# ScalarE's order in a step of an attention kernel: the postmix weights ahead of the copy of the postmix

## The chip, the cores and the metric

One core of one Trainium2 chip. The metric is the time of one execution on the device in microseconds (us); of several executions the median counts.

## What is computed

An attention with two mixes over the heads (2 batches, 12 heads, 448 tokens, 64 channels), then two dense blocks (768 to 2048 to 768) over its 896 rows. The attention is the part that matters here:

```python
scores = scale * np.matmul(q, k.transpose(0, 1, 3, 2))
scores = np.einsum('bhij,hg->bgij', scores, w_pre)
scores = scores - np.max(scores, axis=-1, keepdims=True)
attn = np.exp(scores)
attn = attn / (np.sum(attn, axis=-1, keepdims=True) + 1e-09)
attn = np.einsum('bhij,hg->bgij', attn, w_post)
return np.matmul(attn, v).astype(np.float32)
```

All of it is in float32; products that need it are made of three matmuls over a high and a low part of each operand.

## The kernel before

The attention runs over 8 chunks, four in each batch, three of 120 query rows and one of 88. A chunk is cut into groups of 10 rows x 12 heads = 120 partitions: 12 groups in a long chunk, 9 in a short one, 90 in all. One turn of the loop over groups is a **step**; there are 90, counted by `m`. The order of the work inside a step is written out by hand (a manual schedule), and every engine takes its instructions in that order. In step m stand:

- GpSimd (POOL): `gsplit(m + 2)` (L273 and L275) splits the scores of group m+2 into `sh` and `sl`. Two buffers each, so `sh` of group m+2 follows the matmuls of group m.
- TensorE (PE): `premix(m)` (L285 to L287), three matmuls into the bank `M`; then `postmix(m - 2)` (L320), eight records of matmuls into the bank `A`, whose stationary operand is `e` of group m-2 and whose moving operand is `wr` of group m-2; then, by tables over the steps of a chunk, two heads' scores of the next chunk (L254, bank `sc`), or two heads' product with v of the chunk before (L340, bank `X`), or both, or neither.
- VectorE (DVE): the row maximum of `M` (L289), and for group m-1 the sum's reciprocal (`norm`, L299 and L300), which lands in `st`.
- ScalarE (ACT): `e` = exp of `M` with the maximum as its bias, and the row sums (L291, two records); the copy `at` of the postmix of group m-3 out of its bank (L324; `aposts` holds it from the step before); and `weigh(m - 2)` (L304), the postmix weights divided by the row sum: `wr` = `wq` times the reciprocal of group m-2.

ScalarE has besides these a copy of one `sc` bank (L257), the copies of `X` (L356), and in some steps preparations of q and k (L229, L221), moves of x (L477) and the first piece of a dense block's weights (L408). DVE takes the other half of each (L257, L357, L230, L222, L410 to L416). In the step's text the copy `at` comes first, then `wr`, then the rest; exp stands at the end of what a step hands to ScalarE, apart from the preparations behind it.

The scores of the next chunk go through a staging tile and a DMA on SP's queue (`spread`, L239) into `full`, from which `gsplit` reads; the first `gsplit` of a chunk, two steps ahead of the chunk's first step, needs the DMAs of all heads.

`A` and `M` have two banks each, `wr` two buffers, `e` four. After the loop, the last two groups are finished in a tail written out by hand, with copy and weights in an order of its own.

Of the kernel before, what the change touches and what calls it, by code (L numbers as in the profile page):

```python
# [49 lines left out]
def fused_kernel(  # L50
# [63 lines left out]
    def load_q(C):  # L114
        ns = chunks[C][3] * GR
        t = front.tile([128, NP, CH], F32, tag="qraw", bufs=2, name=f"qraw{C}")
        nc.sync.dma_start(out=t[:, :, :ns], in_=q[C, :, :, :ns])
        qraw[C] = t

    def load_k(b, m):  # L120
        t = front.tile([128, 2, S], F32, tag="raw", bufs=5, name=f"kraw{b}_{m}")
        nc.sync.dma_start(out=t, in_=k[b, :, 2 * m : 2 * m + 2])
        kraw[(b, m)] = t

    def load_v(C, hp):
        if C < len(chunks) - 1:
            t = att.tile([JP, 2, JC * D], F32, tag="vraw", bufs=3, name=f"vraw{C}_{hp}")
            nc.sync.dma_start(out=t, in_=v[chunks[C][0], hp])
            vraw[(C, hp)] = t
# [87 lines left out]
    def k_prep(b, hp):  # L217
        src = kraw[(b, hp // 2)][:, hp % 2, :]
        hi, lo = kst[:, 0, hp, :], kst[:, 1, hp, :]
        preps.append([  # L220
            lambda: nc.scalar.activation(out=hi, in_=src, func=AF.Copy),  # L221
            lambda: nc.vector.tensor_tensor(out=lo, in0=src, in1=hi.bitcast(F32), op=ALU.subtract),  # L222
        ])

    def q_prep(C, p0=0, p1=NP):
        ns = chunks[C][3] * GR
        hi, lo, src = (x[:, p0:p1, :ns] for x in (qr, ql, qraw[C]))
        preps.append([
            lambda: nc.scalar.activation(out=hi, in_=src, func=AF.Copy),  # L229
            lambda: nc.vector.tensor_tensor(out=lo, in0=src, in1=hi.bitcast(F32), op=ALU.subtract),  # L230
        ])
# [9 lines left out]
    def scores(C, hp, tags=("sc", "sc"), st=None):  # L241
        n = chunks[C][3] * GR
        kh, kl = kst[:, 0, hp, :], kst[:, 1, hp, :]
        if hp == 0:
            full[C] = att.tile([GP, MG, S], F32, tag="full", bufs=2, name=f"full{C}")
        room(2)
        sc = [ps.tile([128, 512], F32, tag=t, bufs=BUFS[t], name=f"sc{C}_{2 * hp + i}") for i, t in enumerate(tags)]
        far = st is None
        if far:
            st = front.tile([CH, 2, S], F32, tag="raw", bufs=5, name=f"stg{C}_{hp}")  # L250
        for j, (w, x) in enumerate(((qr, kh), (ql, kh), (qr, kl))):
            for i in range(2):
                o = slice(i * D, i * D + D)
                nc.tensor.matmul(sc[i][:n, :S], lhsT=w[o, hp, :n], rhs=x[o], start=(j == 0), stop=(j == 2))  # L254

        def take(i, copy):
            copy(out=st[:n, i], in_=sc[i][:n, :S])  # L257
            if far:
                spread(C, 2 * hp + i, st[:, i])

        post(2, lambda: take(0, nc.scalar.copy), lambda: take(1, nc.vector.tensor_copy))
# [3 lines left out]
    def gsplit(m, eng=nc.gpsimd):  # L265
        if m >= len(groups):
            return
        C, g = groups[m]
        r = GP
        sh = att.tile([GP, S], F32R, tag="sh", bufs=2, name=f"sh{m}")  # L270
        sl = att.tile([GP, S], F32R, tag="sl", bufs=2, name=f"sl{m}")
        s = full[C][:, g, :]
        eng.tensor_scalar(out=sh[:r], in0=s[:r], scalar1=1.0, scalar2=0.0, op0=ALU.mult, op1=ALU.add)  # L273
        ssp[m] = (sh, sl)
        return eng.tensor_tensor(out=sl[:r], in0=s[:r], in1=sh[:r].bitcast(F32), op=ALU.subtract)  # L275
# [20 lines left out]
    def norm(m):  # L296
        r = GP
        e, st = epx[m]
        nc.vector.tensor_scalar(out=st[:r, 2:3], in0=st[:r, 1:2], scalar1=1e-9, scalar2=None, op0=ALU.add)  # L299
        nc.vector.reciprocal(out=st[:r, 3:4], in_=st[:r, 2:3])  # L300

    def weigh(m):
        wr = att.tile([GP, H, GR], F32, tag="wr", bufs=2, name=f"wr{m}")
        nc.scalar.activation(out=wr, in_=wq, func=AF.Copy, scale=epx[m][1][:, 3:4])  # L304
        wrs[m] = wr
# [23 lines left out]
    def av_unit(C, h):  # L329
        b, r0, n, G = chunks[C]  # L330
        if h % 2 == 0:
            return
        if h % 4 == 1:
            tag = "X" if C + 1 < len(chunks) or h == 1 else "A"
            xps[C] = ps.tile([128, 512], F32, tag=tag, bufs=BUFS[tag], name=f"X{C}_{h}")
        X = xps[C][:, : 2 * CH].rearrange("p (h n) -> p h n", n=CH)
        for jc in range(JC):
            for hh in (h - 1, h):
                vs = vraw[(C, hh // 2)][:, hh % 2, :].rearrange("p (c d) -> p c d", d=D)
                nc.tensor.matmul(  # L340
                    X[hh % 2 * D : hh % 2 * D + D, hh % 4 // 2, :n], lhsT=vs[:, jc, :], rhs=at[C][:, jc, hh, :n],
                    start=(jc == 0), stop=(jc == JC - 1),
                )
        load_v(*((C, h // 2 + 3) if h // 2 + 3 < NP else (C + 1, h // 2 + 3 - NP)))
        if h % 4 == 3:
            av_evac(C, h, X)
# [178 lines left out]
    LAG = 2  # L525
# [8 lines left out]
    m = 0  # L534
    for C, (b, r0, n, G) in enumerate(chunks):
        nxt = C + 1 if C + 1 < len(chunks) else None
        sched = {}

        def add(units, steps):
            for i, u in enumerate(units):  # L540
                sched.setdefault(steps[i * len(steps) // len(units)], []).append(u)

        if nxt is not None:
            add([lambda h=h: scores(nxt, h) for h in range(NP)], SST[G])
        if C + 2 < len(chunks):
            add([lambda: q_prep(C + 2, 0, NP // 2), lambda: q_prep(C + 2, NP // 2, NP)], QST[G])
        if C == NCH - 2:
            add([lambda m=m: load_k(1, m) for m in range(3)], [4, 5, 6])
            add([lambda h=h: k_prep(1, h) for h in range(NP - 1)], [8, 8, 9, 10, 11])
        if C == NCH - 1:  # L550
            add([lambda: k_prep(1, NP - 1)], [0])
        if C > 0:
            add([lambda h=h: av_unit(C - 1, h) for h in range(1, H, 2)], [("av", a) for a in AVST[G]])

        for s in range(G):
            if s == 0 and C + 2 < len(chunks):
                load_q(C + 2)
            if C == 0 and s == 1:
                for i in range(3):
                    load_v(0, i)  # L560
            while aposts:
                aposts.pop(0)()
            if m >= LAG:
                weigh(m - LAG)
            for p in posts + xposts:
                p[0]()
            gsplit(m + 2)
            for p in posts:
                p[1]()
            premix(m)  # L570
            if m >= 1:
                norm(m - 1)
            for p in xposts + lows:
                p[1]()
            for p in preps:
                p[0]()
            lows[:] = preps
            preps.clear()
            xposts.clear()
            posts.clear()  # L580
            banks_of.clear()
            if C > PRE or (C == PRE and s == G - 1):
                next(wpieces)
            if m >= LAG:
                postmix(m - LAG)
            for u in sched.get(("av", s), []):
                u()
            for u in sched.get(s, []):
                u()
            if C == PRE and s == LATE - 1:  # L590
                flush()
                front.release()
                pools["late"] = tc.alloc_tile_pool(name="late", bufs=1, side="right", reuse_waits="tile")
                load_units(1)
                wpieces = (p for u in units[:4] for p in split_pieces(u))
            if C == PRE and s >= LATE:
                x_move(s - LATE, 0, XEAR)
            if C > PRE and s < KD - 3:
                x_move(s + 3, 0, XEAR)
            if C > PRE and s == 3:  # L600
                x_move(slice(0, KD), XEAR, XRAW)
            if C > PRE and s == 1:
                load_vs()
            if C > PRE and s == 4:
                load_units(2)
            if nxt is None and s >= 7:
                if s == 7:
                    h100 = gemm1(0, 0, ps.tile([128, 512], F32, tag="sc", bufs=3, name="h1_0_0"))
                for _ in range(3):
                    next(h100)  # L610
            m += 1
# [265 lines left out]
```

## Time and profile before

| | |
|---|---|
| time, median of 3 executions | 757.08 us (756.6 to 760.44) |
| the profiled execution | 760.78 us, of which the span is 759.1 us |
| mean granted clock of TensorE | 0.984 of full speed |
| PE busy | 719.2 us (95%) |
| DVE, ACT, POOL busy | 537.3, 429.6, 256.1 us (71%, 57%, 34%) |
| chain that ended last | PE 72%, DVE 16%, ACT 5%, DMA 4%, issue 2% |
| attention (steps) | from about 24 to 264 us of the span; the dense blocks follow |

The busy shares are means over stages. "Idle before" is the time an engine stood still ahead of an instruction, and "<-" names what ended it. PE's records last longer than the time they keep the next one back, so a gap in PE's records is less than what PE lost.

### The profile page before, as it was taken

The numbers are of one execution on the slowest core, as the hardware profiler recorded it, in microseconds if no ns is written. First come the engines' busy times: TensorE is split into PE (matmuls) and PEld (weight loads), VectorE is DVE, ScalarE is ACT, GpSimd is POOL, SyncE is SP. The second block draws the span as 40 slices with busy tenths as digits, with TensorE's granted clock in tenths as the row PEclk, the third lists the DMA queues.
The fourth block names the chain that finished last, engine by engine and source line by source line (L and its number), as shares of the span: only waits on it lengthen the run. The fifth ranks groups of instructions, "written<-read, shape, count | busy, mean of one in ns | idle before, by whom it ended". The sixth has DMA issues, their size and how long they took to land.

```text
span 759.1 us, 12175 instructions
## 1 busy us (share of the span) xinstructions
PE 719.2 (95%) x4457; PEld 620.4 (82%) x4457; DVE 537.3 (71%) x947; ACT 429.6 (57%) x869; POOL 256.1 (34%) x255
## 2 busy tenths in 40 slices
PE   5889999999998999999999999999999998999996
PEld 3568777778777788989888888899899887999886
DVE  5455557554545569876755555569999999999996
ACT  4476677676677634344421111247767566689872
POOL 1676665566666535534334444200000000000000
PEclk8799999999999999999999999999999999999999
DMA  6535355444337335334223333333443454401002
GB/s 188 175 103 154 115 178 161 150 150 135 116 118 226 110 97 153 100 108 126 87 94 111 111 110 99 116 106 126 125 132 121 127 162 126 146 21 63 1 1 83
DMA packets 63283, 89.76 MB, mean 118 GB/s; under 512 B 5172, under 2 KB 53880, under 8 KB 63224
## 3 DMA queue, kind: packets, MB, share of 16 engines
q1 hardware_dynamic: 62592, 88.55, 37.9%
q8 instruction: 35, 0.57, 0.3%
q10 hardware_dynamic: 568, 0.43, 0.2%
q14 instruction: 24, 0.20, 0.1%
q0 software_dynamic: 64, 0.01, 0.1%
HBM read 66.87 MB, written 2.75 MB: 92 GB/s over the span
## 4 chain that ended last, share of the span: by engine, by line
PE 72%; DVE 16%; ACT 5%; DMA 4%; issue 2%; SPq 0%; ACTq 0%; DVEq 0%
PE h L366 9%; PE h L364 8%; PE A L320 8%; PE h L365 8%; PE y L364 5%; PE X L340 5%; PE y L365 5%; PE y L366 5%; PE sc L254 5%; PE M L285 4%; PE M L287 2%; PE M L286 2%; PE acc L365 2%; PE acc L366 2%; DVE u L713 2%
## 5 line engine op out<-in xcount | busy, mean ns | idle before, releaser
L364 PE MATMUL h<-xh,wh 128*128 128x512 f32 (+1 forms) x384 | 142.5, 371 | 2.4 <-DVE u L711 1.4
L366 PE MATMUL h<-xh,wl 128*128 128x512 f32 (+1 forms) x384 | 141.4, 369 | 2.1 <-DVE wl L427 2.1
L365 PE MATMUL h<-xl,wh 128*128 128x512 f32 (+1 forms) x384 | 141.2, 368 | 0.0
L408 ACT ACTIVATE wf<-wraw 128x768 f32<-128x768 f32 (+1 forms) x50 | 43.8, 876 | 122.2 <-POOL wl L424 103.6
L320 PEld LDWEIGHTS A<-wr,e 120*112 120x112 f32 x720 | 83.3, 178 | 31.1 <-ACT wr L304 27.7
L289 DVE TENSOR_REDUCE st<-M 120x1 f32<-120x448 f32 x90 | 56.2, 624 | 72.0 <-PE M L287 67.7
L320 PE MATMUL A<-wr,e 120*112 120x120 f32 x720 | 92.7, 272 | 14.8 <-ACT wr L304 14.8
L275 POOL TENSOR_TENSOR sl<-full,sh 120x448 fp32r<-120x448 f32 x89 | 102.4, 1150 | 7.4
L291 ACT ACTIVATE e<-M,st 120x448 f32<-120x448 f32 x90 | 57.2, 635 | 66.4 <-DVE st L289 66.2
L273 POOL TENSOR_SCALAR sh<-full 120x448 fp32r<-120x448 f32 x89 | 53.2, 597 | 88.0 <-PE M L286 56.9
L364 PEld LDWEIGHTS h<-xh,wh 128*128 128x128 f32 x384 | 72.5, 189 | 12.4 <-DVE u L711 2.3
L366 PEld LDWEIGHTS h<-xh,wl 128*128 128x128 f32 x384 | 72.5, 189 | 11.9 <-DVE wl L427 3.3
L410 DVE TENSOR_SCALAR wf<-wf 128x768 int32<-128x768 int32 (+1 forms) x50 | 27.6, 552 | 74.0 <-ACT wf L408 74.0
L365 PEld LDWEIGHTS h<-xl,wh 128*128 128x128 f32 x384 | 72.6, 189 | 8.2
L423 POOL TENSOR_SCALAR wh<-wf 128x768 fp32r<-128x768 f32 (+1 forms) x34 | 33.2, 977 | 130.3 <-PE y L365 56.1
L364 PE MATMUL y<-gh,wh 128*128 128x384 f32 x192 | 70.6, 368 | 0.0
L365 PE MATMUL y<-gl,wh 128*128 128x384 f32 x192 | 70.2, 366 | 0.0
L366 PE MATMUL y<-gh,wl 128*128 128x384 f32 x192 | 69.7, 363 | 0.0
L424 POOL TENSOR_TENSOR wl<-wf,wh 128x768 fp32r<-128x768 f32 (+1 forms) x34 | 65.9, 1939 | 2.8
L324 ACT ACTIVATE at<-A 112x480 f32<-112x480 f32 x90 | 51.7, 574 | 6.3 <-PE A L320 6.2
L416 DVE SCALAR_TENSOR_TENSOR wf<-wraw,icst,wf 128x768 int32<-128x768 int32 (+1 forms) x50 | 51.8, 1038 | 0.8
L412 DVE SCALAR_TENSOR_TENSOR wf<-wraw,icst,wf 128x768 int32<-128x768 int32 (+1 forms) x50 | 50.2, 1003 | 0.8
(113 smaller groups left out, 1522.5 us busy)
## 6 DMA issues: line engine op xcount, KB each, us to landing
wraw<-in_moe_w_in_dram SPq DMA_DIRECT2D x32, 768.0 KB
wraw<-in_moe_w_out_dram SPq DMA_DIRECT2D x28, 768.0 KB
full<-stg SPq DMA_DIRECT2D x60, 210.0 KB
vraw<-in_v_dram SPq DMA_DIRECT2D x42, 224.0 KB
full<-stg SPq DMA_DIRECT2D x24, 157.5 KB
wraw<-in_moe_w_out_dram SPq DMA_DIRECT2D x6, 512.0 KB
kraw<-in_k_dram SPq DMA_DIRECT2D x6, 448.0 KB
qraw<-in_q_dram SPq DMA_DIRECT2D x6, 360.0 KB
```

The costliest lines, as they stand in the source:

```text
L273: eng.tensor_scalar(out=sh[:r], in0=s[:r], scalar1=1.0, scalar2=0.0, op0=ALU.mult, op1=ALU.add)
L275: return eng.tensor_tensor(out=sl[:r], in0=s[:r], in1=sh[:r].bitcast(F32), op=ALU.subtract)
L289: nc.vector.tensor_reduce(out=st[:r, 0:1], in_=mt[:r, :S], op=ALU.max, axis=AX.X, negate=True)
L291: nc.scalar.activation(out=e[:r], in_=mt[:r, :S], func=AF.Exp, bias=st[:r, 0:1], accum_out=st[:r, 1:2])
L320: nc.tensor.matmul(av[:, jc], lhsT=e[:r, jc * JP : (jc + 1) * JP], rhs=wr[:r, :, :rr], start=True, stop=True)
L324: lambda: nc.scalar.activation(out=at[C][:, :, :, c0 : c0 + rr], in_=av, func=AF.Copy)
L364: nc.tensor.matmul(o, lhsT=wh, rhs=mh, start=first, stop=False)
L365: nc.tensor.matmul(o, lhsT=wh, rhs=ml, start=False, stop=False)
L366: nc.tensor.matmul(o, lhsT=wl, rhs=mh, start=False, stop=last)
L412: nc.vector.scalar_tensor_tensor(out=wi, in0=hw, scalar=icst[:, 0:1], in1=wi, op0=ALU.bitwise_and, op1=ALU.bitwise_or)
L416: nc.vector.scalar_tensor_tensor(out=wi, in0=lw, scalar=icst[:, 1:2], in1=wi, op0=ALU.logical_shift_right, op1=ALU.bitwise_or)
L424: nc.gpsimd.tensor_tensor(out=lv, in0=w, in1=hv.bitcast(F32), op=ALU.subtract)
```

## The change

The two statements change places, so that in each step from the third on ScalarE meets the weights `wr` of group m-2 first and the copy `at` of group m-3 right behind them. Nothing else is touched; the tail keeps its order.

```diff
             if C == 0 and s == 1:
                 for i in range(3):
                     load_v(0, i)
+            if m >= LAG:
+                weigh(m - LAG)
             while aposts:
                 aposts.pop(0)()
-            if m >= LAG:
-                weigh(m - LAG)
             for p in posts + xposts:
                 p[0]()
```

The instructions of PE, DVE, POOL and SP stand in the same order as before. ScalarE's order at the end of the fifth chunk, around the stall that the prediction follows (numbers behind names are the group; a leading + is the new place, a leading - the old one):

```order
 L291 ACTIVATE e67_2572,st67_2570<-M67_2566,st67_2570 120x448
 L229 ACTIVATE qr_123<-qraw7_2209 128x3x90
+L304 ACTIVATE wr66_2584<-wq_60,st66_2536 120x120
 L324 ACTIVATE at5_2301<-A65_2579 112x48x10
-L304 ACTIVATE wr66_2585<-wq_60,st66_2536 120x120
```

The weights of group 66 move over one copy; exp of group 67 and the preparation of q stay ahead of both.

ScalarE's order at the passage from the first chunk to the second (group 12 is the second chunk's first):

```order
 L291 ACTIVATE e10_549,st10_547<-M10_543,st10_547 120x448
 L229 ACTIVATE qr_123<-qraw2_246 128x360
+L304 ACTIVATE wr9_560<-wq_60,st9_524 120x120
 L324 ACTIVATE at0_323<-A8_555 112x48x10
-L304 ACTIVATE wr9_561<-wq_60,st9_524 120x120
 L291 ACTIVATE e11_573,st11_571<-M11_567,st11_571 120x448
+L304 ACTIVATE wr10_585<-wq_60,st10_547 120x120
 L324 ACTIVATE at0_323<-A9_578 112x48x10
-L304 ACTIVATE wr10_586<-wq_60,st10_547 120x120
 L291 ACTIVATE e12_598,st12_596<-M12_592,st12_596 120x448
```

Between one exp and the next only the pair of weights and copy has turned round, in each step alike.

## Rows read from the trace of the kernel before

**Rows 1.** The page, busy time of each engine over the span.
```profile
PE 719.2 (95%) x4457; PEld 620.4 (82%) x4457; DVE 537.3 (71%) x947; ACT 429.6 (57%) x869; POOL 256.1 (34%) x255
```
**Rows 2.** Windows: span; PE, PEld, DVE, ACT, POOL busy (instructions); clock, DMA share, GB/s.
```profile
46.00:145.00 99.00, 93.21 (x807) 73.12 (x806) 56.99 (x149) 70.10 (x188) 62.41 (x73) 1.00 0.48 143
145.00:245.00 100.00, 94.80 (x833) 74.99 (x834) 53.35 (x150) 71.59 (x191) 67.18 (x78) 1.00 0.50 149
...
330.00:420.00 90.00, 90.00 (x440) 79.76 (x439) 55.93 (x76) 30.21 (x48) 34.52 (x25) 1.00 0.33 104
```
**Rows 3.** Waits over the span: who for whom, us in total, times, longest.
```profile
ACT e L291 <- DVE st L289: 66.2, 77, 5.7
...
PEld A L320 <- ACT wr L304: 27.7, 44, 1.7
...
PE A L320 <- ACT wr L304: 14.8, 21, 1.4
```
**Rows 4.** Timeline 200 to 212 us, a stall: start, duration, engine, line, operation [idle before].
```profile
200.48 0.19 ACT L291 ACTIVATION_READ_ACCUMULATOR e<-M,st 120x1 f32 x1
200.53 0.37 PE L287 MATMUL M<-sl,wp_h 120*120 120x448 f32 x1
200.57 0.42 ACT L229 ACTIVATE qr<-qraw 128x270 fp32r<-128x270 f32 x1
...
200.89 0.57 ACT L324 ACTIVATE at<-A 112x480 f32<-112x480 f32 x1
...
201.35 0.39 ACT L304 ACTIVATE wr<-wq,st 120x120 f32<-120x120 f32 x1
...
201.62 0.63 ACT L291 ACTIVATE e<-M,st 120x448 f32<-120x448 f32 x1
...
201.78 1.07 PE L320 MATMUL A<-wr,e 120*112 120x120 f32 x8 [0.89 <-ACT wr L304]
```
**Rows 5.** The same timeline, two steps without a stall of PE.
```profile
206.21 0.16 DVE L300 RECIPROCAL st<-st 120x1 f32<-120x1 f32 x1
...
206.78 0.57 ACT L324 ACTIVATE at<-A 112x480 f32<-112x480 f32 x1
...
207.24 0.39 ACT L304 ACTIVATE wr<-wq,st 120x120 f32<-120x120 f32 x1
...
207.68 0.89 PEld L320 LDWEIGHTS A<-wr,e 120*112 120x112 f32 x8 [0.21 <-ACT wr L304]
207.69 1.06 PE L320 MATMUL A<-wr,e 120*112 120x120 f32 x8
...
210.17 0.99 PE L320 MATMUL A<-wr,e 120*112 120x120 f32 x8
```
**Rows 6.** Timeline 44 to 55 us, passage from the first chunk to the second.
```profile
47.74 1.07 PE L320 MATMUL A<-wr,e 120*112 120x120 f32 x8 [0.33 <-ACT wr L304]
...
49.42 0.57 POOL L273 TENSOR_SCALAR sh<-full 120x448 fp32r<-120x448 f32 x1 [2.49 <-PE M L286]
...
50.02 1.07 PE L320 MATMUL A<-wr,e 120*112 120x120 f32 x8 [0.59 <-ACT wr L304]
50.08 1.14 POOL L275 TENSOR_TENSOR sl<-full,sh 120x448 fp32r<-120x448 f32 x1
...
51.34 0.39 PE L287 MATMUL M<-sl,wp_h 120*120 120x448 f32 x1
...
52.04 1.07 PE L320 MATMUL A<-wr,e 120*112 120x120 f32 x8 [0.31 <-ACT wr L304]
```
**Rows 7.** Windows about the one stretch of lower clock in the later steps.
```profile
245.00:248.00 3.00, 2.18 (x23) 1.49 (x22) 1.22 (x6) 2.72 (x7) 2.83 (x4) 1.00 0.38 105
250.00:252.00 2.00, 1.54 (x8) 1.54 (x8) 1.80 (x4) 1.14 (x4) 2.00 (x2) 0.63 0.51 174
252.00:254.00 2.00, 2.00 (x18) 1.58 (x17) 0.00 (x0) 0.85 (x2) 1.41 (x2) 0.52 0.00 0
```
**Rows 8.** Timeline 245 to 256 us, PE alone: the same matmuls at both clocks.
```profile
250.46 1.92 PE L320 MATMUL A<-wr,e 120*112 120x120 f32 x8 [0.61 <-ACT wr L304]
252.31 1.81 PE L340 MATMUL X<-at,vraw 112*64 112x120 f32 x16
...
254.77 0.98 PE L320 MATMUL A<-wr,e 120*112 120x120 f32 x8
```

## The prediction

> **What bounds the kernel now.** I read the page's busy times first, then windows by stage, then the waits, then the timeline around single waits. TensorE is busy for 95% of the span [rows 1]. The windows show where the rest is: in the 199 us of steps from 46 to 245 us PE's records leave 5.8 and 5.2 us open, while in the first dense block, 330 to 420 us, there is no gap at all [rows 2]. So the attention is bound by PE too, apart from short holes, and time taken out of a hole moves all that follows, since PE behind it is full. What ends those holes is in the list of waits: PE stood before the postmix for ScalarE's weights `wr` 21 times, 14.8 us together; the loading of the postmix's stationary operand (PEld) waited for it 44 times, 27.7 us [rows 3]. That is the largest wait of PE in these steps, and the wait that this change is about. ScalarE itself has room: before exp it stands 66.2 us in 77 waits for VectorE's maximum [rows 3].
>
> One stall in full [rows 4]: ScalarE ends the sums of exp and a preparation of q, takes the copy `at` at 200.89 us, starts `wr` 0.46 us behind it at 201.35, and PE starts the postmix at 201.78, 0.43 us after `wr` started, having stood 0.89 us. The copy feeds nothing that PE does next. It is simply ahead in the queue.
>
> **The change, part by part.**
>
> *`wr` starts earlier by one copy.* The copy lasts 0.57 us, but the next instruction starts 0.46 us behind its start [rows 4, 5]. `wr` needs the reciprocal, which in the step of rows 5 ends at 206.37, 0.41 us before the copy's start at 206.78, so it can take the copy's place at once. Each `wr` therefore comes 0.46 us earlier. The Trainium skill ("ScalarE: Activation LUTs", section "What ACT_TABLE_LOAD costs") gives 186 ns + 0.833 ns an element for an activation without pointer operands and an overlap of about 93 ns between two in a row; an estimate from that for this copy of 480 columns is 0.49 us, and with it the term below would be 0.4 us larger. The rows decide: 0.46.
>
> *Stalls of PE.* Not all 21 pay 0.46. The postmix of step m waits for `wr`, which is behind the exp of step m-1, whose `M` was made on PE ahead of the postmix of step m-1. A gain in one stall thus does not reach the `wr` of the next step, only that of the second next, and a stall that directly follows another (within ScalarE's or VectorE's unbroken run of work) is shortened by nothing new: PE comes earlier by as much as `wr` does. I went through the 21 by their starts. Twelve stand alone or come first of their run (31.09, 38.41, 79.92, 109.54, 121.55, 139.67, 148.59, 168.51, 201.78, 233.25, 239.72 and 248.15 us). Each was long enough for 0.46, counting that PE's records run on some 0.2 us past the point where the next could start. That is 12 x 0.46 = **5.5 us**. Five follow in a run and give nothing (112.01, 116.18, 170.92, 241.74, 250.46).
>
> *The passage from the first chunk to the second* has the other four (45.72 to 52.04 us) and is the one place where another wait stands close behind. POOL's `sh` for the second chunk starts at 49.42 after 2.49 us of idleness; the row names PE, but the matmul it names was long done for the group in question, so I take it that the DMA of the second chunk's scores had just landed. `sl` ends at 51.22 and PE's matmul on it starts at 51.34 [rows 6]. These four stalls would give 1.2 us by the rule above, but the matmul at 51.34 can then move by 0.1 us only beyond what the DMA gained from earlier stalls. What is left is the hole between it and the postmix at 52.04: 0.70 us, of which 0.2 is the matmul itself. I take **0.5 us**. At later passages 16 or 32 matmuls with v stand in between, and `sl` is ready more than 0.4 us ahead.
>
> *Weight loads without a stall of PE.* In 44 - 21 = 23 steps PEld waited, mostly 0.2 us, while PE's records show no gap. There the eight postmix matmuls take 1.06 us, against 0.99 where the load was not held up [rows 5], so 0.07 us each: 23 x 0.07 = **1.6 us**. The Trainium skill says otherwise: by "TensorE: Matmul & The Clock Gate", section "Step-by-step: what each phase is for", the PE queue pulls weight loads ahead of matmuls in flight, and this load reads `e`, not `wr`; by that rule the load would be done already and this term nil, leaving 6.0 us. The trace does not agree: the load itself stands until `wr` is there [rows 5].
>
> *What is made later.* The copy `at` starts about 0.28 us later than now (the distance from `wr` to the instruction after it: 201.35 to 201.62 in rows 4). It empties a bank of `A` that PE fills again a step later, over 2 us on; its reader, the product with v, stands on PE behind the postmix, which lasts longer than the copy. The copies of `sc` and exp behind the pair start when they did, since the pair takes the same time in either order; where `at` used to wait for PE's last postmix, `wr` no longer waits with it. So I cost this at nothing; the cover is ScalarE's 66.2 us before exp [rows 3], and without it 87 steps x 0.28 would be at stake.
>
> *Sum:* 5.5 + 0.5 + 1.6 = 7.6 us off the profiled execution's 760.78, which makes 753.2. That execution lies 3.7 us above the median of the three, as does the slowest of them; the holes I count belong to any execution, so I take the 7.6 off the median: 757.08 - 7.6 = **749.5 us**.
>
> *Bounds.* From above: all 21 stalls at 0.46 (9.7), the weight loads, and the clock of the second rival: 12.9 us, 744.2. From below: the weight loads nil and half of the stalls' 6.0 given back: 3 us, 754.
>
> **Rivals.**
>
> *The stall moves to another wait.* Once `wr` is early, the next thing that is late is the split `sl` on POOL or, at a chunk's end, the DMA of the scores, as in rows 6. If that held at all seven passages, up to one 0.46 each (3.2 us) and the 0.5 would be lost and 3.9 us stay: 753.2. For it: rows 6. Against it: PE's waits for `sl` are not among the large ones. Chance 0.15.
>
> *The clock stays up as well.* After the stalls around 240 to 250 us the granted clock is 0.63 and then 0.52, which is the 1.2 GHz level; the postmix takes 1.92 us instead of 1.07 and the next 16 matmuls with v 1.81 instead of 1.04: 1.6 us [rows 7, 8]. PE was busy for 2.18 of the 3 us from 245 to 248. With shorter holes the fall may not come: 749.5 - 1.6 = 747.9. The Trainium skill ("TensorE: Matmul & The Clock Gate", section "What's actually happening") has it that the throttled clock is the default and that activity releases it; by that rule the fall goes. That 46 to 245 us, with holes of 11 us in all, kept full clock [rows 2] speaks for it as well. Against: the holes here shrink, they do not close. Chance 0.15.
>
> *It does nothing to PE.* If PE's holes are only put down to `wr` and the postmix is held by something that ends at the same moment, the time stays at 757. The 0.43 us from `wr`'s start to PE's, the same in each stall I looked at, speaks against it. Chance 0.07.
>
> *Slower: `wr` now waits for VectorE, with the copy and exp queued behind it.* Today the copy covers the reciprocal's lateness; the margin is 0.41 us [rows 5]. If the reciprocal came late by d beyond that margin in every step, copy and exp would be d later in 87 steps, and with exp the next maximum. It costs 87 x d and decides against the change from d = 0.09; slower by more than 0.5% from d = 0.13, for instance 761 us. The reciprocal stands on VectorE right behind the maximum that exp waits for, so it is early whenever exp is; hence 0.03.
>
> **How the numbers follow.** Forecast 0.60, the rivals 0.15, 0.15, 0.07 and 0.03. A difference of 0.5% (3.8 us) is about what a measurement of this kernel tells from none. Faster by more: the forecast, the clock and half of the first rival, 0.83; within: the other half and the third, 0.14; slower 0.03. The range goes from 744.5, near the bound above, to 754.0, the bound below, and leaves out the last two rivals.
>
> **What would show it.** In the changed profile: PE's waits for `wr` fall from 14.8 to about 8 us and from 21 to fewer; PEld's from 27.7 and 44 times to about 13; each lone stall is shorter by 0.46, 0.89 at 201.78 becoming about 0.4; the last postmix of the steps comes some 7.6 us earlier, and the dense blocks last as long as before. The forecast is wrong if the waits fall and the last postmix does not move, which would be the first rival, or if exp's waits turn from the maximum to ScalarE's own queue.

## The result and the profile after

The changed kernel takes 751.16 us (median of 6, 750.45 to 752.37) against 757.6 us for the kernel before (median of 6): 6.4 us faster, where 7.6 had been forecast. The ratio on record is not that of the two medians; it is 0.9902, with a 95% interval of 0.9882 to 0.9921, which is 7.4 us of 757.6 (6.0 to 8.9). The forecast lies inside this interval. With the runs below, too, the microseconds are differences of medians, and the ratio on record can lie up to 1.1 us from them. The profiled executions, 750.68 and 760.78 us, lie 10.1 us apart; what that has to do with the timed difference is explained below with e0.

Busy time on the page of the changed kernel [rows 1]:

```profile
PE 715.0 (95%) x4457; PEld 621.4 (83%) x4457; DVE 533.2 (71%) x947; ACT 427.9 (57%) x869; POOL 258.0 (34%) x255
```

The counts of instructions are the same as before [rows 1]. PE's busy time is 4.2 us lower, but 3.5 of these are missing in a second profile of the kernel before as well (e0 below, PE busy for 715.7 us); most of what the change took out is idle time. Windows of the changed kernel over the steps and the first dense block [rows 2], and the waits [rows 3]:

```profile
46.00:140.00 94.00, 90.40 (x793) 72.48 (x792) 52.48 (x147) 68.04 (x184) 62.65 (x72) 1.00 0.49 146
140.00:237.00 97.00, 93.63 (x834) 76.50 (x834) 53.73 (x150) 71.02 (x190) 67.43 (x78) 1.00 0.53 154
...
262.00:420.00 158.00, 158.00 (x770) 140.05 (x770) 111.25 (x144) 58.10 (x93) 66.56 (x44) 1.00 0.35 109
```

```profile
ACT e L291 <- DVE st L289: 60.5, 75, 6.0
...
PEld A L320 <- ACT wr L304: 16.1, 22, 1.3
...
PE A L320 <- ACT wr L304: 8.1, 14, 0.9
```

PE's wait for `wr` fell from 14.8 to 8.1 us and from 21 times to 14, the weight load's from 27.7 to 16.1 and from 44 times to 22. PE's gaps in the steps fell from 11.0 us in 199 to 7.0 in 191.

The stall of rows 4, in the timeline of the changed kernel:

```profile
194.02 0.19 ACT L291 ACTIVATION_READ_ACCUMULATOR e<-M,st 120x1 f32 x1
194.11 0.42 ACT L229 ACTIVATE qr<-qraw 128x270 fp32r<-128x270 f32 x1
194.43 0.38 ACT L304 ACTIVATE wr<-wq,st 120x120 f32<-120x120 f32 x1
194.72 0.56 ACT L324 ACTIVATE at<-A 112x480 f32<-112x480 f32 x1
194.87 1.07 PE L320 MATMUL A<-wr,e 120*112 120x120 f32 x8 [0.64 <-ACT wr L304]
195.18 0.62 ACT L291 ACTIVATE e<-M,st 120x448 f32<-120x448 f32 x1
```

`wr` starts right behind the preparation of q. From exp's sums to PE's postmix it is 194.87 - 194.02 = 0.85 us, before 201.78 - 200.48 = 1.30: 0.45 less. Exp of the next group still starts 1.16 us behind the sums (1.14 before), so the pair's turn cost exp nothing. Two of the forecast's signs came out weaker than stated: the weight load's waits, 16.1 us in 22 times where about 13 us were forecast, and the gap ahead of this stall, 0.64 us where about 0.4 was. PE now reaches this stall 0.21 us behind the sums (194.87 - 0.64 - 194.02) and not 0.41 (201.78 - 0.89 - 200.48), so the gap is only 0.25 us shorter although the postmix starts 0.45 sooner.

### The profile page after: what moved, and what is told of

Read it like the earlier page. It is cut to its first block, busy times and chain, and to the rows that moved or that the text cites. A ratio compares the mean times of both kernels' runs of the same rounds, so it can differ in the third digit from the quotient of the medians.

```text
span 749.0 us, 12177 instructions
## 1 busy us (share of the span) xinstructions
PE 715.0 (95%) x4457; PEld 621.4 (83%) x4457; DVE 533.2 (71%) x947; ACT 427.9 (57%) x869; POOL 258.0 (34%) x255
## 4 chain that ended last, share of the span: by engine, by line
PE 74%; DVE 15%; ACT 4%; DMA 4%; issue 2%; SPq 1%; POOL 0%; ACTq 0%; POOLq 0%; DVEq 0%
PE h L364 9%; PE h L366 9%; PE h L365 9%; PE A L320 8%; PE X L340 5%; PE y L364 5%; PE y L365 5%; PE y L366 5%; PE sc L254 5%; PE M L285 4%; PE M L287 2%; PE acc L365 2%; PE M L286 2%; PE acc L366 2%; PE acc L364 2%
## 5 line engine op out<-in xcount | busy, mean ns | idle before, releaser
L320 PEld LDWEIGHTS A<-wr,e 120*112 120x112 f32 x720 | 85.1, 176 | 19.6 <-ACT wr L304 16.1
L320 PE MATMUL A<-wr,e 120*112 120x120 f32 x720 | 90.3, 268 | 8.4 <-ACT wr L304 8.1
```

Of the source, the lines that this page charges most:

```text
L320: nc.tensor.matmul(av[:, jc], lhsT=e[:r, jc * JP : (jc + 1) * JP], rhs=wr[:r, :, :rr], start=True, stop=True)
```

## The experiments

**e1 and e2: the two halves of the steps.** e1 puts the weights first only in the 21 steps with a stall of PE, e2 only in the 66 others. The cut shows e1; `STALLED` stands for the list of the 21 steps that its code spells out.

```diff
-            if m >= LAG:
+            if m >= LAG and m in STALLED:
                 weigh(m - LAG)
             while aposts:
                 aposts.pop(0)()
+            if m >= LAG and m not in STALLED:
+                weigh(m - LAG)
```

e1: 

> The weights stand ahead of the copy only in the 21 steps in which PE stood before the postmix in the profile of before; in the other 66 the old order. Theory (a stall of PE ends one copy, 0.46 us, sooner, and the stalls alone carry most of it): 5 to 6 us faster than before, ratio about 0.993, PE's wait for wr about 8 us as in the changed kernel, PEld's about 20 us, since the 23 short waits of the weight load stay. Rival (every step gains a little, ScalarE's line being shorter everywhere): 21 of 87 steps would give a quarter of the 6.4 us, 1.6 us, ratio 0.998.

Measured: 752.22 us against 758.35, ratio 0.9919 (0.9906 to 0.9933), 6.1 us faster.

e2: 

> The complement: weights first in the 66 other steps, the old order in the 21 with a stall of PE. Theory: only the weight load's short waits go, 23 x 0.07 = 1.6 us, ratio 0.998; PE's wait for wr stays near 14.8 us and PEld's falls by about 5 us. Rival (every step gains): three quarters of 6.4 us, 4.8 us, ratio 0.9937. With e1 the two should add up to the 6.4 us of the whole change.

Measured: 757.37 us against 758.35, ratio 0.9988 (0.9976 to 0.9999), 1.0 us faster. The waits of e1, then of e2:

```profile
PEld A L320 <- ACT wr L304: 20.2, 43, 1.3
...
PE A L320 <- ACT wr L304: 7.7, 16, 0.9
```

```profile
PEld A L320 <- ACT wr L304: 23.9, 22, 1.7
...
PE A L320 <- ACT wr L304: 15.6, 21, 1.3
```

The rival of an even gain is out: a quarter of the steps carries 6.1 us, three quarters carry 1.0. e1 keeps the many short waits of the weight load (43) and halves PE's; e2 does the reverse (22, and PE's 15.6 us stay). Together 7.1 us, against 6.4 for the whole change by the medians and 7.4 by the ratio, within the intervals.

**e3: the weights ahead of the preparations too.**

```diff
-            if m >= LAG:
-                weigh(m - LAG)
...
             if m >= 1:
                 norm(m - 1)
+                weigh(m - 1)
```

The cut is against the kernel before; behind the loop the tail's own `weigh(m - 2)` goes as well, since its group is done by then.

> The weights of group m-1 are issued right behind exp of step m, ahead of the preparations of q and k, the moves of x, the first weight piece and the copy of the next step. The remaining stalls of the changed kernel (8.1 us, 14 times) stand mostly behind such a preparation of 0.3 to 1.4 us. Theory (ScalarE's line between exp and wr sets the stall): some 4 to 5 us off the changed kernel, about 746.5 us, ratio to before about 0.986, PE's wait for wr down to 3 to 4 us. Rival (what is left of the stalls hangs on POOL's splits, the DMA or VectorE): no more than 1 us off the changed kernel, the waits reappearing under those names.

Measured: 749.25 us against 758.35, ratio 0.9873 (0.986 to 0.9886). That is 9.1 us below the kernel before, but only 1.9 below the changed kernel by the medians, where 4 to 5 were expected: the size was missed. Its waits:

```profile
PEld A L320 <- ACT wr L304: 10.2, 13, 1.4
...
PE A L320 <- ACT wr L304: 5.2, 13, 1.0
```

The mechanism is there (8.1 to 5.2 us, 16.1 to 10.2), though PE's wait stays above the 3 to 4 us expected. Between the start of the second chunk and the end of the steps its trace gains 3.7 us on the changed kernel's, from 1.2 behind to 2.5 ahead at the last postmixes. The 1.2 behind come from the start: in the profile of e3 TensorE's clock is at its lower level, 1.2 GHz, until about 31 us, in that of the changed kernel until about 26. The windows of e3, then of the changed kernel, then of e8 (below), which up to this point is the changed kernel:

```profile
28.00:30.00 2.00, 2.00 (x11) 1.88 (x10) 0.85 (x4) 0.62 (x3) 1.49 (x2) 0.50 0.60 147
30.00:32.00 2.00, 2.00 (x13) 1.82 (x12) 0.54 (x1) 0.93 (x4) 0.97 (x3) 0.68 0.86 266
```

```profile
26.00:28.00 2.00, 2.00 (x11) 0.93 (x9) 1.43 (x4) 0.85 (x3) 1.64 (x2) 0.95 0.43 131
```

```profile
30.00:32.00 2.00, 2.00 (x13) 1.74 (x11) 0.67 (x2) 0.83 (x4) 0.97 (x3) 0.72 0.85 267
```

The late rise belongs to the one execution and not to e3's order: e8 has it too, and e7 (below), which up to this point is e3, has its rise at about 26 us. How much of the missing gain in the timed executions is the clock's is not shown; e3's four were granted 0.983 to 0.986 of full speed in the mean, the changed kernel's six 0.986 to 0.989.

**e0: the kernel before once more** (unchanged).

> The kernel before once more, with a profile. Its profiled execution was 3.7 us above the median and the granted clock fell at 250 us. If that fall belongs to single executions, this profile lacks it, the span is near 755 to 756 us, and the waits for wr are 14 to 15 us again; if it belongs to the kernel, the stretch about 250 to 254 us is at half clock again.

Measured: 757.77 us, span 756.1; PE's wait for `wr` 14.0 us, 19 times. The stretch of rows 8, in the timeline of e0, and its window [rows 7]:

```profile
249.71 1.07 PE L320 MATMUL A<-wr,e 120*112 120x120 f32 x8 [0.62 <-ACT wr L304]
250.71 1.04 PE L340 MATMUL X<-at,vraw 112*64 112x120 f32 x16
252.39 0.98 PE L320 MATMUL A<-wr,e 120*112 120x120 f32 x8
```

```profile
250.00:252.00 2.00, 2.00 (x26) 1.70 (x25) 1.05 (x2) 1.36 (x4) 1.92 (x3) 1.00 0.07 21
```

The clock did not fall, with the same stalls ahead of it (1.00 and 0.62 us, against 0.97 and 0.61). The fall belonged to one execution. From 250.46 to 254.77 the earlier profile took 4.31 us for what took 2.68 here: 1.6 us that no execution has by necessity.

Against e0 the changed kernel's profile starts the last postmix of the steps at 255.96 us, not at 264.01, 8.05 us sooner where some 7.6 were forecast. About 0.9 of that is not the change's. The first postmix of all, ahead of which no copy stood that could change places, already starts 0.60 us sooner, and the next one gains 0.77 us where it gained 0.46 in e1: the clock rose at about 26 us in the changed kernel's profile and between 28 and 29 in those of e0 and e1.

Behind the steps 0.95 us is lost again, so that the span is 7.1 us shorter (749.0 and 756.1). There the clock fell to its lower level twice in the changed kernel's profile, at about 623 and 733 us, and not at all in e0's. The windows ahead of the first fall and at it in the changed kernel, then those 7 us later in e0, about the same work:

```profile
615.00:623.00 8.00, 5.32 (x26) 4.16 (x25) 7.53 (x14) 5.83 (x9) 0.00 (x0) 1.00 0.33 98
623.00:627.00 4.00, 4.00 (x15) 4.00 (x16) 3.96 (x6) 0.00 (x0) 0.00 (x0) 0.57 0.13 16
```

```profile
622.00:630.00 8.00, 6.64 (x32) 5.15 (x30) 7.64 (x14) 6.96 (x11) 0.00 (x0) 1.00 0.45 144
630.00:634.00 4.00, 2.70 (x15) 2.70 (x16) 4.00 (x6) 0.00 (x0) 0.00 (x0) 1.00 0.01 4
```

The order on ScalarE does not decide it: of the two profiles of the kernel before, one has both falls and e0 neither. From the start of the last postmix to the end, the five profiles here without such a fall (e0, e2, e4, e7, e8) take 491.6 to 492.1 us, the seven with it 492.7 to 494.9.

**e4: the change turned round.** The weights stand behind the copies of `sc` and `X`.

```diff
-            if m >= LAG:
-                weigh(m - LAG)
             while aposts:
                 aposts.pop(0)()
             for p in posts + xposts:
                 p[0]()
+            if m >= LAG:
+                weigh(m - LAG)
```

> The change turned the other way: the weights stand behind the copy of the postmix and also behind the copies of sc and X, as the last of the step's first group on ScalarE. In some 40 steps a copy of sc (about 0.43 us of ScalarE's line) and in 21 a copy of X (about 0.27 us) now precedes them. Theory (each us ahead of wr that PE's own work does not cover is a us of PE, over two steps): the cover in steps with scores is at most 0.1 us, so about 0.4 us are lost in every two steps, 8 to 14 us slower than before, ratio 1.011 to 1.018, and PE's wait for wr rises from 14 to over 20 us. Rival (the gain of the change came from something else than the place of wr, the order of copy and exp say): within 2 us of before.

Measured: 772.73 us against 758.33, ratio 1.0183 (1.0161 to 1.0205): 14.4 us slower, just above the 8 to 14 that were expected. Timeline of e4, and its waits:

```profile
192.71 0.58 ACT L324 ACTIVATE at<-A 112x480 f32<-112x480 f32 x1
193.17 0.53 ACT L257 COPY stg<-sc 120x448 f32<-120x448 f32 x1
193.58 0.41 ACT L304 ACTIVATE wr<-wq,st 120x120 f32<-120x120 f32 x1
194.04 0.89 PEld L320 LDWEIGHTS A<-wr,e 120*112 120x112 f32 x8 [0.62 <-ACT wr L304]
194.05 1.07 PE L320 MATMUL A<-wr,e 120*112 120x120 f32 x8 [0.23 <-ACT wr L304]
```

```profile
PEld A L320 <- ACT wr L304: 46.5, 76, 1.6
...
PE A L320 <- ACT wr L304: 14.6, 28, 1.2
```

Each copy ahead of `wr` costs PE. One part of the expectation failed: PE's own wait, expected at over 20 us, stayed at 14.6 although 14 us were lost. The loss shows in the weight load's wait, 46.5 us in 76 of 90 steps.

**e5: the copy further back,** behind the copies of `sc` and `X`, the weights first.

```diff
             if m >= LAG:
                 weigh(m - LAG)
-            while aposts:
-                aposts.pop(0)()
             for p in posts + xposts:
                 p[0]()
+            while aposts:
+                aposts.pop(0)()
```

> The changed kernel with the copy of the postmix moved one place further back, behind the copies of sc and X; the weights stay first. Theory (the copy has cover until PE fills its bank again a step later): the time of the changed kernel within 1.5 us, ratio to before 0.990 to 0.993, waits for wr as there. Rival (the late copy costs something, which took a part of the forecast 7.6 us): 2 us or more above the changed kernel, with PE waiting for at before the product with v or for a bank of A.

Measured: 751.18 us against 758.33, ratio 0.9891 (0.9866 to 0.9916), the changed kernel's time. The copy's lateness is covered, as the forecast had costed it.

**e6, e7, e8, e9: the passage to the second chunk.** In the changed kernel's timeline stands the wait for `sl` that the forecast had expected here:

```profile
47.39 0.56 POOL L273 TENSOR_SCALAR sh<-full 120x448 fp32r<-120x448 f32 x1 [2.16 <-DMA qraw<-in_q_dram]
...
48.04 1.38 POOL L275 TENSOR_TENSOR sl<-full,sh 120x448 fp32r<-120x448 f32 x1
...
49.48 0.47 PE L287 MATMUL M<-sl,wp_h 120*120 120x448 f32 x1 [0.61 <-POOL sl L275]
```

e6 moves the second chunk's last scores a step forward, e7 is e3 with that, e8 is the changed kernel with a later load of q, e9 is e7 with that.

```diff
-            add([lambda h=h: scores(nxt, h) for h in range(NP)], SST[G])
+            add([lambda h=h: scores(nxt, h) for h in range(NP)], SST[G] if C else [0, 1, 3, 4, 5, 6])
```

```diff
-            if s == 0 and C + 2 < len(chunks):
+            if s == (2 if C == 1 else 0) and C + 2 < len(chunks):
                 load_q(C + 2)
```

e6: 

> The changed kernel, with the last two score pairs of the second chunk made in steps 5 and 6 of the first chunk in place of 6 and 7, so that their DMAs leave a step earlier. In the changed kernel PE waited 0.61 us for POOL's sl at the passage to the second chunk. Theory (that wait hangs on the DMA of those scores): the wait is gone, POOL's sh for the second chunk starts about 2 us earlier against the matmuls around it, and the time falls by up to 1 us, less what the emptier step 7 gives PE to wait for wr. Rival (the wait hangs on POOL's own rate): it stays at 0.5 us or more.

e7: 

> e3 and e6 together: weights right behind exp, and the second chunk's last scores a step earlier. e3 lost 0.6 us at the passage to the second chunk in its profile. Theory: the passage no longer takes back what the first chunk gains, about 1 to 1.5 us below e3, 748 us, ratio 0.986. Rival (something later, the clock at the start or POOL, sets the passage): the time of e3 within 0.5 us.

e8: 

> The changed kernel, with the load of the fourth chunk's q (270 KB) two steps later, so that in SP's queue it no longer follows right behind the DMAs of the second chunk's scores. In e6 those DMAs left earlier, and the wait for sl stayed, while the DMA engines were over 0.9 busy until sh started. Theory (sh waits for the engines' throughput, and the q load shares it): without the q load the DMA engines fall idle about 1 us earlier, sh of the second chunk starts some 1 us earlier against the last issue of the scores' DMAs (3.8 us in the changed kernel), PE's 0.61 us wait for sl at the passage goes or falls under 0.2 us; the time falls by 0.6 us at most, which the timing cannot tell. Rival (the DMAs of the scores take as long without it): the distance and the wait stay.

e9: 

> e7 with the q load of e8: weights right behind exp, the second chunk's last scores a step earlier, the q load two steps later. Theory: the passage costs nothing more, up to 0.5 us below e7, so 745 to 746 us and ratio 0.982 to 0.984. Rival (the passage was already free in e7, or something else sets it): the time of e7.

Measured: e6 750.73 us against 758.33, ratio 0.989 (0.9871 to 0.9909), the changed kernel's time. e7 745.62 against 758.33, 0.983 (0.9808 to 0.9851), 3.6 us below e3 by the medians, where 1 to 1.5 were expected. e8 749.57 against 759.14, 0.9887 (0.9859 to 0.9915). e9 746.64 against 759.14, 0.9838 (0.9818 to 0.9857), e7's time. PE's matmul on `sl` and POOL's `sh` at the passage, in e6, e7, e8 and e9:

```profile
47.02 0.57 POOL L273 TENSOR_SCALAR sh<-full 120x448 fp32r<-120x448 f32 x1 [2.57 <-DMA qraw<-in_q_dram]
...
49.02 0.47 PE L287 MATMUL M<-sl,wp_h 120*120 120x448 f32 x1 [0.70 <-POOL sl L275]
```

```profile
46.33 0.57 POOL L273 TENSOR_SCALAR sh<-full 120x448 fp32r<-120x448 f32 x1 [1.39 <-DMA qraw<-in_q_dram]
...
48.18 0.46 PE L287 MATMUL M<-sl,wp_h 120*120 120x448 f32 x1
```

```profile
47.78 0.56 POOL L273 TENSOR_SCALAR sh<-full 120x448 fp32r<-120x448 f32 x1 [1.34 <-PE A L320]
...
49.93 0.37 PE L287 MATMUL M<-sl,wp_h 120*120 120x448 f32 x1
```

```profile
47.07 0.56 POOL L273 TENSOR_SCALAR sh<-full 120x448 fp32r<-120x448 f32 x1 [2.02 <-DMA full<-stg]
...
49.15 0.46 PE L287 MATMUL M<-sl,wp_h 120*120 120x448 f32 x1 [0.79 <-POOL sl L275]
```

e6's expectation failed: the DMAs left 2 us sooner (the last was issued by 41.4 us, not 43.6), `sh` came 0.4 us sooner and the wait stayed. The wait stayed as its rival had it, but not for the rival's reason, since POOL stood 2.57 us waiting for a DMA. e8 went as its theory had it, the wait was gone; but e9 has no q load in this place either, and PE waited 0.79 us, while e7 has it and PE did not wait. So the q load is not the cause, at least not alone. e9 was expected up to 0.5 us below e7 and did not go below it.

The packed traces tell which transfer it was, by the times at which its parts landed. In e0, the changed kernel, e6, e7, e8 and e9 alike, `sh` starts 0.26 us behind the last landing of the scores' transfer that was issued last (in the changed kernel 47.13 and 47.39 us). The q load, which the row names, landed in full only at 47.78 us, when `sh` was already running, so the row's name is wrong there. In the changed kernel this last transfer was issued at 42.83 us and took 4.30 us to its last landing; in e6 it was issued at 40.64, 2.2 us sooner, and took 6.12. In e7 it took 5.30 us, in e9 4.91 and in e8 3.47. In e9's windows the DMA engines moved 204 to 231 GB/s up to 45 us:

```profile
44.00:45.00 1.00, 0.74 (x5) 0.33 (x3) 0.41 (x3) 1.00 (x4) 1.00 (x1) 1.00 0.64 231
45.00:46.00 1.00, 0.94 (x9) 0.94 (x10) 0.97 (x4) 1.00 (x4) 0.05 (x1) 1.00 0.14 50
46.00:47.00 1.00, 0.94 (x6) 0.53 (x5) 0.31 (x2) 1.00 (x4) 0.00 (x0) 1.00 0.02 7
```

Twelve transfers of 210 KB at such a rate take some 11 us (an estimate from these windows) whenever the last one is issued, and a thin rest of them lands after 46 us. What sets the end of that rest to within a microsecond stays open.

e7 is, with e9, the best of the versions run: 12.7 us below the kernel before. Its 3.6 us on e3 are not the passage's alone. Its profile is 4.3 us shorter than e3's, and by the starts of the postmix the four steps of the passage give 1.0 of that, as the theory had it. Of the rest, 1.4 us are gained at the first two postmixes, where the clock is up in e7 and not yet in e3, and 2.4 behind the steps, where e3's clock falls twice and e7's never; 0.5 is lost in between.

## Why the prediction was right, point by point

*What bounds it.* Right: PE, by holes that `wr` ends. e4 shows the same from the other side.

*0.46 us a copy.* Right: 0.45 in the stall shown. The Trainium skill ("ScalarE: Activation LUTs", section "What ACT_TABLE_LOAD costs") leads to an estimate of 0.49; the trace stays with the smaller one.

*Stalls.* Forecast, with the passage, 6.0 us; e1 measured 6.1 (5.1 to 7.1). By the start of the postmix in the two profiles, the twelve stalls that were counted gave between 0.12 and 0.77 us each, 5.3 in all, and four of the five that were counted at nothing gave 0.10 or less. The fifth, at 116.18, gave 0.66, but there e0 is ahead of the earlier profile by the same 0.66, so it is a matter of the execution. Of the 0.77, at 31.09, some 0.3 is the clock's (see e0), and against e0 the stalls at 121.55 (with the step ahead of it) and 148.59 gave 0.3 each. So the 5.5 came to about 5, and this is the term that was too large. Two stalls, at 79.92 and 201.78, gave only some 0.35: a weight load in the step ahead had already gained 0.10, which lies inside the 0.46 and not on top of it. e1, which leaves that weight load as it was, gains the full 0.46 at both, and e2, which takes it out alone, loses the 0.10 again at both. The forecast's sum counted these 0.2 us twice.

*The passage.* Right in size and mechanism: about 0.6 us where the rule for stalls would have given 1.2, with `sl` as the next wait, 0.61 us. That only the first passage does so held: the wait of 0.61 us is the only one of PE for POOL's `sl` in the whole profile. The first rival was thus confined to one place.

*Weight loads.* Forecast 1.6; e2 measured 1.0 (0.1 to 1.8), which is barely clear of nothing and does not rule out 1.6. The traces are sharper. By the starts of the postmix 20 steps without a stall gained 0.04 to 0.15 us each against e0, 1.5 us together, both in the changed kernel and in e2; in e1, which keeps the waits of the weight load, the same 20 gained 0.2 together. Such a step of the changed kernel, to be held against the last two rows of rows 5 (2.48 us from start to start, now 2.41):

```profile
200.76 0.98 PE L320 MATMUL A<-wr,e 120*112 120x120 f32 x8
...
203.17 0.98 PE L320 MATMUL A<-wr,e 120*112 120x120 f32 x8
```

So the term was about right. The rule of the Trainium skill ("TensorE: Matmul & The Clock Gate", section "Step-by-step: what each phase is for") that weight loads are pulled ahead, by which the term would be nil, is thus not borne out here: the load stood until `wr` was there, and taking these waits out gave 1.5 us.

*The copy at nothing.* Right (e5). Nor did `wr` come to wait for VectorE, the rival that would have made the kernel slower: ScalarE stands idle ahead of no `wr` in either profile.

*From the sum to the median.* Right to have left the profile's extra 3.7 us out. 1.6 of it was the fall of the clock at 250 us, which e0 lacks. The second rival, a clock that stays up because of the change, falls: the kernel before keeps it up too.

Between the 7.6 us of the forecast and the 6.4 of the medians no further cause is needed, since 7.6 lies inside the interval of the ratio. In the traces the gain by the last postmix of the steps against e0, 8.05 us, less the 0.9 that the clock gave at the start, is 7.1; these are two profiles, one execution each. Against the forecast's sign the part behind the steps took 0.95 us longer than in e0. That goes with the falls of the clock there, which come and go between executions.

## What to carry to other kernels

On an engine that takes its work in order, sort by who waits: what another engine needs next goes ahead of what only frees a buffer. Here such a swap was worth the start-to-start distance of the instruction passed over, once for each run of stalls, not once for each stall, because the next wait of a run was set two steps back. Count the stalls on the queue that loads weights too, but do not add a gain there to that of a stall in the next step, and look for the transfer or split that is late next. Before a difference of a microsecond between two profiles is put down to a change, compare the granted clock of both, stretch by stretch.

## What the runs showed of the hardware that was not expected

A gap in PE's records is a poor measure of what PE loses: in e4 14.4 us went, while PE's wait for `wr` stayed at 14.6 us (14.0 in e0) and the weight load's rose from 27.1 to 46.5. TensorE's clock fell to half at 250 us in one profile of the kernel before and not in another, behind stalls of the same length. At the start it rose at about 26 us in one profile and 31 in another, with the same work issued up to there (the changed kernel and e8). In the dense blocks it fell in seven of the twelve profiles and not in five, and once more both are found with one and the same kernel.
